# Pooled attention into a rational mixture layer on one core: the first keys on 96 partitions, the first queries by halves of the heads, the first values' first addition on GpSimd, and the order of the work planned anew

## The chip, the core and the metric

The kernel runs on one NeuronCore of a Trainium2 chip. Five engines work side by side and meet only through semaphores: TensorE (PE in the profile; its weight loads are PEld), VectorE (DVE), ScalarE (ACT), GpSimd (POOL) and SyncE (SP), which here only issues transfers. Sixteen DMA engines move the data. The metric is the device time of one execution in microseconds, lower being better: the median of the runs of a kernel.

## The reference, cut to what matters

Attention over eight batches, with keys and values averaged over groups of eight rows first, and a layer with a rational function between two products after it:

```python
B, H, S, D = 8, 8, 576, 64          # Sp = S // 8 = 72 pooled rows
k_p = k.reshape(B, H, Sp, 8, D).mean(axis=3)
v_p = v.reshape(B, H, Sp, 8, D).mean(axis=3)
scores = q @ k_p.transpose(0, 1, 3, 2) / sqrt(D)
attn = exp(scores - max); attn = attn / (sum(attn) + 1e-9)
x = (attn @ v_p), heads side by side: 4608 tokens x 512
h = x @ w_in                                            # 512 -> 2048
P = a0 + a1 h + a2 h^2 + a3 h^3
Q = 1 + |b0| |h| + |b1| h^2
out = (P / (Q + 1e-6)) @ w_out                          # 2048 -> 512
```

The two weight arrays arrive as 64-bit floats and are read as pairs of 32-bit words; everything else is 32-bit.

## The kernel before, in words

The 4608 tokens are cut into 18 blocks of 256 (`NBLK`). Each block goes through three stages: attention (`attend`), then for each of 8 units `u` of 256 hidden columns the first product (`mm1`, result `ph` in a PSUM bank), the rational function (`rational`, tiles `t`, `w`, `r`, `rp`, `gh`, `gl` on ACT, DVE and POOL) and the second product (`mm2`, result `po`). Both products are made of three matmuls each on a high and a low part, so TensorE has far more work than any other engine. Each of the 18 blocks costs TensorE the same; nothing in the change adds to or takes from the products.

**What sets the order.** The functions do not issue instructions. They record operations in a `Plan`, each with an engine, an estimated cost and a due time (`plan.now`), and `solve` then builds one list: at each step the engine that can start first takes, among the operations that could start within `LOOK` of the earliest, the one due first. `slack`, `early`, `lead`, `HEAD`, `SLOW`, the offsets of `plan.now` in `attend`'s and `mm1`'s calls are the planner's rules; changing one can move instructions everywhere. `issue` then writes every engine's instructions in that order, all on one line of the file (L299 before, L303 after), so the profile is read by tile names. Each engine runs its own list strictly in order: an instruction that waits holds all that stand behind it.

**Fillers.** Where the planner expects TensorE to be idle, `issue` writes matmuls that compute nothing (L290 before, L294 after): into the bank `idle` before the first products, later additions of zero to a `po` bank. They only keep TensorE occupied.

**The head.** The first 40 us or so are special. Block 0 is computed in two halves of four heads each (`c` = 0 and 1): `first_keys(c)` loads and pools the keys of batch 0 for these heads (tile `early` at place 0 or 3, sums on DVE, transposed on PE into `pk`, copied to `kpT`), `first_half(c)` transposes the queries (`pq`, `qT`), forms the scores (`ps`), their maxima (`mx`), the exponentials (`e`), the sums (`sm`), the product `e*sm` on POOL, and the transposed weights (`pm`, `pr`, tiles `am`); `values(0)` multiplies by the pooled values (`pv`, split into a high and a low `x`). `prep_v_early(0)` loads the values of batch 0 in two halves (`early` at place 2), adds the upper half of each row group to the lower, and sums the other steps on PE (`pvs`, and `pvr` for the remaining rows). Block 1 needs batch 0 too, block 2 needs the keys and values of batch 1 (`prep_k(1)`, `prep_v_early(1)`: the later `early`, `pk`, `pvs`, `pvr`). In between the weights are loaded (`rwin`, `rwout`), decoded (`m_win` on ACT and DVE) and split (`win`: the high part on ACT, the low one on POOL).

In this trace SyncE's queue has one ring of transfers for all of this, issued in the order of the list.

Of the kernel before, what the change touches and what calls it, by code (L numbers as in the profile page):

```python
# [100 lines left out]
class Plan:  # L101
# [8 lines left out]
    LOOK = 0.02  # L110
# [6 lines left out]
    def __init__(self, nc):  # L117
        self.nc, self.ops, self.rings, self.now, self.slack = nc, [], {}, 0.0, 2.4
# [10 lines left out]
    def add(self, eng, cost, calls, port=False, claims=(), bytes=0, early=38, after=()):  # L129
        op = Op()  # L130
        op.eng, op.cost, op.port, op.calls, op.bytes = eng, cost, port, calls, bytes
        op.early, op.slack, op.lead = early, self.slack, 0.0
        op.seq, op.due, op.deps, op.users = len(self.ops), self.now, set(), []
        touched = {}
        for _, args, kw in calls:
            every = list(args) + list(kw.values())
            dst = kw.get("out", args[0] if args else None)
            for v in every:
                if isinstance(v, Lazy) and v is not dst:
# [4 lines left out]
            if isinstance(dst, Lazy):  # L144
# [174 lines left out]
def tile_pooled_attention_then_rational_moe(  # L319
# [21 lines left out]
    G = 8  # L341
# [8 lines left out]
    SQ = 4  # L350

# [23 lines left out]
    def bank(name, shape):  # L375
        return new("ps", "ps", shape, F32, name)
# [3 lines left out]
    gp = Engine(plan, "pool", 0.242, 2.021)  # L380

# [125 lines left out]
    def prep_k(n):  # L507
# [5 lines left out]
        for c0, c1, np in ((0, 2, P), (2, 4, P), (4, 5, H * SP - 4 * P)):  # L513
# [25 lines left out]
            turned.lead = 0.75 if n > 2 else 0.0  # L539
# [18 lines left out]
    def first_keys(c):  # L558

        place = early(0, 3 * c)[:SP].rearrange("p (h x) -> p h x", h=4)  # L560
        dma(4 * SP * 2, place, k[0, 4 * c:4 * c + 4].rearrange("h (s t) d -> s h (t d)", t=G))
        pk = bank(f"pk0_{c}", [P, 2, SP])
        w = RW // 2
        while w > D:
            dve(4 * w, port=True).tensor_tensor(
                out=place[:, :, 0:w], in0=place[:, :, 0:w], in1=place[:, :, w:2 * w], op=ALU.add)
            w //= 2
        ks = new("work1", "ks", [P, 2, 2, D], F32, f"ks0_{c}")[:SP].rearrange(
            "p a b d -> p (a b) d")
# [5 lines left out]
        act(2 * SP).activation(kpT[0][0:D, js, 0:SP], pk[0:D], AF.Copy, scale=1.0 / G)  # L575
        dve(2 * SP).tensor_scalar(out=kpT[0][D:P, js, SP:2 * SP], in0=pk[D:P], scalar1=1.0 / G,
                                  scalar2=None, op0=ALU.mult)
# [5 lines left out]
    def prep_v_early(n):  # L583
# [5 lines left out]
        if n == 0:  # L589
            for c in range(2):  # L590
                js = slice(2 * c, 2 * c + 2)
                half = early(0, 2)[:, c * CW:(c + 1) * CW].rearrange("p (j x) -> p j x", j=2)
                dma(512, half, rows[js, REM:, :].rearrange("j r x -> r j x"))
                dve(RW, port=True).tensor_tensor(
                    out=half[:, :, 0:RW // 2], in0=half[:, :, 0:RW // 2],
                    in1=half[:, :, RW // 2:RW], op=ALU.add)
                for t in range(0, G // 2, 2):
                    pe(430, [mm(vs[:, js], ident, half[:, :, s * D:(s + 1) * D], s == 0,
                                s == G // 2 - 1) for s in range(t, t + 2)], claims=(vs,))
        else:  # L600
# [10 lines left out]
        w = RW // 2 if n == 0 else 0  # L611
# [4 lines left out]
        if n == 0:  # L616
            pe(250, [mm(vrs, fourfold, st[:, 0], True, True)])
        for s in range(0, G if n else 0, 2):
# [155 lines left out]
    def first_half(c, hi, lo, qt, qT, es):  # L774

        js = slice(2 * c, 2 * c + 2)
        mx = new("work2", "mx", [P, H], F32, f"mx0_{c}").rearrange(
            "p (j t h) -> p j t h", t=2, h=2)
        sm = new("work2", "sm", [P, H], F32, f"sm0_{c}")
        for t in range(2):  # L780
            pq = bank(f"pq0_{t}_{c}", [P, 2, P])
            pe(110 * 2, [
                ("transpose", (pq[:, j, :], qt[t][:, 4 * c + 2 * j:4 * c + 2 * j + 2, :].rearrange(
# [5 lines left out]
               claims=(es, mx, sm))  # L789
            dve(4 * SP).tensor_reduce(out=mx[:, :, t, :],  # L790
                                      in_=ps.rearrange("p (j h) s -> p j h s", h=2),
                                      op=ALU.max, axis=AX.X)
# [3 lines left out]
                in1=mx[:, :, t, :].unsqueeze(3).to_broadcast([P, 2, 2, SP]), op=ALU.subtract)  # L796
        act(8 * SP).activation(es[:, js], es[:, js], AF.Exp, scale=D ** -0.5)
        e = es[:, js].rearrange("p j t (h s) -> p (j t h) s", s=SP)
        dve(8 * SP).tensor_reduce(out=sm, in_=e, op=ALU.add, axis=AX.X)
# [56 lines left out]
    def attend(i):  # L856
# [64 lines left out]
    def mm1(i, u, xs):  # L921
# [5 lines left out]
        for h, cs in enumerate(parts):  # L927
            plan.now += 8 * h
# [8 lines left out]
        plan.now -= 8 * h  # L937
# [90 lines left out]
    order += [(i, u) for u0 in (0, NA) for i in (2, 3) for u in range(u0, u0 + NA)]  # L1028
# [19 lines left out]
    for at, (i, u) in enumerate(order):  # L1048
        again = i < 2 and u >= NA
        plan.now = due(at)  # L1050
        if (i, again) not in xs:
            plan.slack = 1.4
            plan.now = due(at) - (0 if again else {1: 9, 2: 8, 3: 11}.get(i, 0.0))
# [3 lines left out]
            if i < 2 and not again:  # L1057

                plan.now = due(at + 6)
# [7 lines left out]
        plan.now = due(at + LAG) + 3  # L1067
# [45 lines left out]
```

## Time and profile before

| | |
|---|---|
| median of 3 runs | 940.88 us (940.12 to 941.06) |
| the profiled execution | 941.77 us, of it the span that the trace covers 940.1 us |
| instructions in the trace | 17117 |
| DVE, ACT, POOL busy, share of the span | 81%, 72%, 56% |
| granted TensorE clock, mean | 0.998 |

A row of the timeline gives start and length in us, engine, line, operation, output and inputs, shape, a count, and in brackets the engine's idle time just before it with what ended it. A row of the windows gives for one stretch the busy time of each engine, then the granted clock (1.00 is full), the mean busy share of the DMA engines and the rate of the transfers.

### The profile page before, as it was taken

The numbers are of one execution on the slowest core, as the hardware profiler recorded it, in microseconds if no ns is written. First come the engines' busy times: TensorE is split into PE (matmuls) and PEld (weight loads), VectorE is DVE, ScalarE is ACT, GpSimd is POOL, SyncE is SP. The second block draws the span as 40 slices with busy tenths as digits, with TensorE's granted clock in tenths as the row PEclk, the third lists the DMA queues.
The fourth block names the chain that finished last, engine by engine and source line by source line (L and its number), as shares of the span: only waits on it lengthen the run. The fifth ranks groups of instructions, "written<-read, shape, count | busy, mean of one in ns | idle before, by whom it ended". The sixth has DMA issues, their size and how long they took to land.

```text
span 940.1 us, 17117 instructions
## 1 busy us (share of the span) xinstructions
PE 929.1 (99%) x6158; PEld 845.3 (90%) x6158; DVE 763.6 (81%) x1335; ACT 677.6 (72%) x1126; POOL 530.8 (56%) x474
## 2 busy tenths in 40 slices
PE   7999999999999999999999999999999999999998
PEld 7899999989999999999999899999999899999996
DVE  6889987688879777878888788878886988787764
ACT  3788888667677767776776867686867786777764
POOL 5776788685447544445644574457543754444452
PEclk9999999999999999999999999999999999999999
DMA  9995201163233412122603160215212231202000
GB/s 282 306 378 176 46 29 46 40 161 87 47 79 76 115 24 58 26 59 51 141 9 70 41 155 10 39 41 129 69 27 53 68 80 23 57 1 58 1 23 23
DMA packets 185072, 75.32 MB, mean 80 GB/s; under 512 B 162332, under 2 KB 162332, under 8 KB 184988
## 3 DMA queue, kind: packets, MB, share of 16 engines
q1 hardware_dynamic: 184988, 74.23, 30.9%
q8 instruction: 49, 0.80, 0.4%
q14 instruction: 35, 0.29, 0.1%
HBM read 50.59 MB, written 12.58 MB: 67 GB/s over the span
## 4 chain that ended last, share of the span: by engine, by line
PE 95%; DMA 3%; SPq 2%; issue 0%; ACT 0%
PE po L299 43%; PE ph L299 43%; PE pv L299 4%; PE ps L299 4%; SPq L299 2%; DMA early<-in_v_dram 1%; DMA q<-in_q_dram 1%; PE pvs L299 1%; PE pk L299 0%; PE pvr L299 0%; PE pq L299 0%; PE pm L299 0%; PE po L290 0%; PE pr L299 0%; PE pl L299 0%
## 5 line engine op out<-in xcount | busy, mean ns | idle before, releaser
L299 PEld LDWEIGHTS ph<-x,win 128*128 128x128 f32 x3264 | 484.4, 188 | 61.7 <-DVE x L299 0.5
L299 PE MATMUL ph<-x,win 128*128 128x256 f32 x3264 | 507.5, 282 | 0.5 <-DVE x L299 0.3
L299 PE MATMUL po<-wout,gh 128*128 128x512 f32 x1152 | 356.9, 396 | 0.0
L299 POOL TENSOR_TENSOR w<-w,r 128x512 f32<-128x512 f32 (+1 forms) x145 | 193.8, 1336 | 269.9 <-ACT r L299 268.2
L299 POOL TENSOR_TENSOR gl<-t,gh 128x512 fp32r<-128x512 f32 (+1 forms) x145 | 190.8, 1316 | 79.5 <-ACT gh L299 78.2
L299 PEld LDWEIGHTS po<-wout,gh 128*128 128x128 f32 x1152 | 182.3, 189 | 7.8 <-issue 0.4
L299 PE MATMUL po<-wout,gl 128*128 128x512 f32 x576 | 181.7, 396 | 0.0
L299 DVE SCALAR_TENSOR_TENSOR t<-t,abn,rp 128x512 f32<-128x512 f32 (+1 forms) x145 | 106.9, 738 | 51.8 <-ACT rp L299 50.0
L299 ACT ACTIVATE t<-ph,abn 128x512 f32<-128x512 f32 (+1 forms) x145 | 112.2, 774 | 40.7 <-PE ph L299 30.2
L299 DVE TENSOR_TENSOR t<-t,ph 128x512 f32<-128x512 f32 (+1 forms) x145 | 97.8, 676 | 41.9 <-ACT t L299 41.0
L299 ACT ACTIVATE r<-w,abn 128x512 f32<-128x512 f32 (+1 forms) x145 | 117.7, 812 | 13.3 <-POOL gl L299 6.6
L299 ACT ACTIVATE w<-ph 128x512 f32<-128x512 f32 (+1 forms) x145 | 86.1, 594 | 54.8 <-PE ph L299 34.8
L299 ACT ACTIVATE rp<-w 128x512 f32<-128x512 f32 (+1 forms) x145 | 86.6, 597 | 41.8 <-POOL w L299 40.1
L299 ACT CAST gh<-t 128x512 fp32r<-128x512 f32 (+1 forms) x145 | 88.8, 613 | 37.7 <-DVE t L299 36.9
L299 DVE SCALAR_TENSOR_TENSOR t<-t,abn,ph 128x512 f32<-128x512 f32 (+1 forms) x145 | 106.4, 735 | 2.4
L299 DVE SCALAR_TENSOR_TENSOR t<-rp,t 128x512 f32<-128x512 f32 (+1 forms) x145 | 98.4, 679 | 2.4
L299 DVE SCALAR_TENSOR_TENSOR rp<-w,rp 128x512 f32<-128x512 f32 (+1 forms) x145 | 98.8, 681 | 0.3
L299 PEld LDWEIGHTS po<-wout,gl 128*128 128x128 f32 x576 | 89.5, 188 | 2.2 <-issue 0.2
L299 ACT ACTIVATE rp<-rp 128x512 f32<-128x512 f32 (+1 forms) x145 | 84.1, 580 | 2.6
L299 POOL TENSOR_TENSOR e<-e,sm 128x576 f32<-128x576 f32 x36 | 42.0, 1186 | 20.4 <-DVE sm L299 14.3
L299 PE MATMUL pv<-am,vm 128*128 128x256 f32 (+3 forms) x288 | 45.9, 279 | 0.0
L299 PEld LDWEIGHTS pv<-am,vm 128*128 128x128 f32 x288 | 41.9, 192 | 0.4
(109 smaller groups left out, 849.6 us busy)
## 6 DMA issues: line engine op xcount, KB each, us to landing
am<-e SPq DMA_DIRECT2D x224, 48.0 KB, 2.1
out_dram<-ob SPq DMA_DIRECT2D x17, 512.0 KB, 3.1
rwin<-in_moe_w_in_dram SPq DMA_DIRECT2D x8, 1024.0 KB, 10.1
rwout<-in_moe_w_out_dram SPq DMA_DIRECT2D x8, 1024.0 KB, 10.5
st_k<-in_k_dram SPq DMA_DIRECT2D x12, 512.0 KB, 4.7
st_v<-in_v_dram SPq DMA_DIRECT2D x12, 512.0 KB, 3.9
q<-in_q_dram SPq DMA_DIRECT2D x144, 32.0 KB, 1.9
st_v<-in_v_dram SPq DMA_DIRECT2D x48, 64.0 KB, 2.2
```

Source lines behind the costliest of these rows:

```text
L299: getattr(engines[op.eng], name)(*map(value, args), **{k: value(v) for k, v in kw.items()})
```

## The change

**The keys of `first_keys`.** Before, a half's 4 heads x 72 pooled rows lie on 72 partitions, four pieces of 2 KB each from four places. Now the 288 rows are dealt to 96 partitions, three consecutive rows of 2 KB (6 KB in one piece) on each. The additions run over 3 rows instead of 4; the last one writes each sum twice side by side (`twice`), three transposes of 96 columns replace two of 72, and the two copies into `kpT` read with a stride of three.

**Block 0's queries.** Two transfers of all 8 heads (one for each 128 tokens) become four of 4 heads.

**The first values' first addition** moves from DVE to GpSimd (`V1E`); the count of matmuls after it is the same.

**The planner.** `LOOK` 0.02 to 0.04, `slack` 2.4 to 2.2 in the beginning, `early` 38 to 54, one `lead` 0.75 to 0.25, and the due times of blocks 1 to 3, of the spills, of the second half of `mm1` and of the rational function. The first maxima get tiles of their own. Options that are added and stay off (`EXPS`, `V1BS`, `REST`, `ORD`) build nothing.

```diff
-    LOOK = 0.02
+    LOOK = 0.04
...
-        self.nc, self.ops, self.rings, self.now, self.slack = nc, [], {}, 0.0, 2.4
+        self.nc, self.ops, self.rings, self.now, self.slack = nc, [], {}, 0.0, 2.2
...
-    def add(self, eng, cost, calls, port=False, claims=(), bytes=0, early=38, after=()):
+    def add(self, eng, cost, calls, port=False, claims=(), bytes=0, early=54, after=()):
...
+    MODE = 0, 1, 0
+    ORD, EXPS = 0, 0
+    V1BS, REST = 0, 0
...
+    V1B = [(), (gp,), (dve,), (gp, gp), (gp, dve)][V1BS]
+    K1E, V1E, K1W = (dve, gp)[MODE[0]], (dve, gp, None)[MODE[1]], (D, RW // 4, RW // 2)[MODE[2]]
...
-            turned.lead = 0.75 if n > 2 else 0.0
+            turned.lead = 0.25 if n > 2 else 0.0
...
     def first_keys(c):
-        place = early(0, 3 * c)[:SP].rearrange("p (h x) -> p h x", h=4)
-        dma(4 * SP * 2, place, k[0, 4 * c:4 * c + 4].rearrange("h (s t) d -> s h (t d)", t=G))
-        pk = bank(f"pk0_{c}", [P, 2, SP])
-        w = RW // 2
+        rows = 4 * SP // 3
+        place = early(0, 3 * c)[:rows, 0:3 * RW].rearrange("p (r x) -> p r x", r=3)
+        dma(2 * 4 * SP, place, k[0, 4 * c:4 * c + 4].rearrange(
+            "h (s t) d -> (h s) (t d)", t=G).rearrange("(p r) x -> p r x", r=3), run=6144)
+        pk = bank(f"pk0_{c}", [P, 3, rows])
+        w, adder = RW // 2, (dve, K1E)[c]
         while w > D:
-            dve(4 * w, port=True).tensor_tensor(
+            adder(3 * w, port=True).tensor_tensor(
                 out=place[:, :, 0:w], in0=place[:, :, 0:w], in1=place[:, :, w:2 * w], op=ALU.add)
             w //= 2
-        ks = new("work1", "ks", [P, 2, 2, D], F32, f"ks0_{c}")[:SP].rearrange(
-            "p a b d -> p (a b) d")
-        dve(4 * w, port=True).tensor_tensor(
-            out=ks, in0=place[:, :, 0:w], in1=place[:, :, w:2 * w], op=ALU.add)
-        pe(110 * 2, [("transpose", (pk[:, j, :], ks[:, 2 * j:2 * j + 2, :].rearrange(
-            "p h d -> p (h d)"), ident[:SP, :SP]), {}) for j in range(2)])
+        twice, both = place[:, :, 2 * D:4 * D], [rows, 3, 2, D]
+        adder(6 * D, port=True).tensor_tensor(
+            out=twice.rearrange("p r (m d) -> p r m d", m=2),
+            in0=place[:, :, 0:D].unsqueeze(2).to_broadcast(both),
+            in1=place[:, :, D:2 * D].unsqueeze(2).to_broadcast(both), op=ALU.add)
+        pe(110 * 3, [("transpose", (pk[:, r], twice[:, r], ident[:rows, :rows]), {})
+                     for r in range(3)])
...
-                dve(RW, port=True).tensor_tensor(
-                    out=half[:, :, 0:RW // 2], in0=half[:, :, 0:RW // 2],
-                    in1=half[:, :, RW // 2:RW], op=ALU.add)
+                if V1E:
+                    V1E(RW, port=True).tensor_tensor(
+                        out=half[:, :, 0:RW // 2], in0=half[:, :, 0:RW // 2],
+                        in1=half[:, :, RW // 2:RW], op=ALU.add)
...
             def start(c):
                 first_keys(c)
-                for t in range(2 - 2 * c):
-                    dma(2 * P, qt[t], q[0, :, t * P:(t + 1) * P, :].rearrange("h s d -> s h d"),
-                        run=256)
+                hs = slice(4 * c, 4 * c + 4)
+                for t in range(2):
+                    dma(P, qt[t][c], q[0, hs, t * P:(t + 1) * P, :].rearrange(
+                        "h s d -> s h d"), run=256)
...
-            plan.now = due(at) - (0 if again else {1: 9, 2: 8, 3: 11}.get(i, 0.0))
+            plan.now = due(at) - (0 if again else {1: 12, 2: 6, 3: 12}.get(i, 0.0))
...
-                plan.now = due(at + 6)
+                plan.now = due(at + 8)
...
-        plan.now = due(at + LAG) + 3
+        plan.now = due(at + LAG) + 5
```

Over the whole program the instructions are the same but for these: 81 fillers into `idle` become 75, 14 additions of zero to `po` become 1, 4 transposes into `pk` become 6, two additions go from DVE to POOL, and the transfers of the first keys and queries are cut as told.

What the new plan moves shows on three engines. The first place is SyncE's list at the start; `early_0` and `early_3` are the first keys, `early_1` the remaining rows of the values (16 partitions) and `early_2` the values' two halves. Before:

```order
L299 DMA early_0_96<-in_k_dram 72x4x512
L299 DMA early_3_98<-in_k_dram 72x4x512
L299 DMA q_106<-in_q_dram 128x8x64 x2
L299 DMA early_1_116<-in_v_dram 16x2x512 x2
L299 DMA early_2_127<-in_v_dram 128x2x512
L299 DMA rwin_134<-in_moe_w_in_dram 128x4x512
L299 DMA early_2_127<-in_v_dram 128x2x512
L299 DMA rwin_156<-in_moe_w_in_dram 128x4x512
L299 DMA fourfold<-in_moe_a_dram 1x4
L299 DMA rwin_212<-in_moe_w_in_dram 128x4x512
L299 DMA rwout_225<-in_moe_w_out_dram 128x2x1024
L299 DMA q_236<-in_q_dram 128x8x64 x2
```

After:

```order
L303 DMA early_0_96<-in_k_dram 96x1536
L303 DMA early_3_98<-in_k_dram 96x1536
L303 DMA q_105<-in_q_dram 128x4x64 x4
L303 DMA early_1_126<-in_v_dram 16x2x512 x2
L303 DMA early_2_140<-in_v_dram 128x2x512 x2
L303 DMA rwin_162<-in_moe_w_in_dram 128x4x512
L303 DMA rwin_196<-in_moe_w_in_dram 128x4x512
L303 DMA fourfold<-in_moe_a_dram 1x4
L303 DMA rwin_214<-in_moe_w_in_dram 128x4x512
L303 DMA q_225<-in_q_dram 128x8x64 x2
L303 DMA rwout_241<-in_moe_w_out_dram 128x2x1024
```

The second half of the values now goes ahead of the first weights, and block 1's queries (`q_236`, now `q_225`) ahead of the first `rwout`.

The second place is POOL from the end of its masks to block 1's softmax; `e_249` and `e_250` are block 0's weights, `e_497` and `e_459` block 1's. Before:

```order
L299 TENSOR_TENSOR early_1_116<-early_1_116 32x4x2x64
L299 TENSOR_TENSOR early_1_116<-early_1_116 32x2x2x64
L299 TENSOR_TENSOR early_1_116<-early_1_116 32x2x64
L299 TENSOR_TENSOR e_249<-e_249,sm_0_276 128x576
L299 TENSOR_TENSOR e_249<-e_249,sm_1_317 128x576
L299 TENSOR_TENSOR win_359<-m_win_274,win_359 128x1024
L299 TENSOR_TENSOR win_441<-m_win_353,win_441 128x1024
L299 TENSOR_TENSOR early_0_272<-early_0_272 128x2x256 x2
L299 TENSOR_TENSOR win_471<-m_win_419,win_471 128x1024
L299 TENSOR_TENSOR e_497<-e_497,sm_526 128x4x144
```

After:

```order
L303 TENSOR_TENSOR early_1_126<-early_1_126 32x4x2x64
L303 TENSOR_TENSOR early_1_126<-early_1_126 32x2x2x64
L303 TENSOR_TENSOR early_2_140<-early_2_140 128x2x256 x2
L303 TENSOR_TENSOR early_1_126<-early_1_126 32x2x64
L303 TENSOR_TENSOR e_250<-e_250,sm_0_278 128x576
L303 TENSOR_TENSOR e_250<-e_250,sm_1_297 128x576
L303 TENSOR_TENSOR win_361<-m_win_300,win_361 128x1024
L303 TENSOR_TENSOR win_453<-m_win_356,win_453 128x1024
L303 TENSOR_TENSOR early_0_260<-early_0_260 128x2x256 x2
L303 TENSOR_TENSOR e_459<-e_459,sm_491 128x4x144
```

The values' two additions stand ahead of block 0's first `e*sm`, and the third `win` no longer stands ahead of block 1's `e*sm`.

The third place is PE's list around block 1's transposed weights (`pm_591` before, `pm_550` after). Before:

```order
L299 MATMUL ph_2_552<-x_0_405,win_471 128x256 x8
L299 MATMUL ph_2_552<-x_0_412,win_471 128x256 x4
L299 MATMUL pm_591<-identr,e_497 128x128 x4
L299 MATMUL ph_2_552<-x_0_405,win_471 128x256 x4
L299 MATMUL pm_604<-identr,e_497 128x128 x4
L299 MATMUL pr_613<-identr,e_497 128x128 x2
L299 MATMUL pr_623<-identr,e_497 128x128 x2
L299 MATMUL pvs_629<-early_2_433,identr 128x256 x4
L299 MATMUL pv_0_646<-am_1_602,vm_324 128x256
```

After:

```order
L303 MATMUL ph_1_486<-x_0_402,win_453 128x256 x4
L303 MATMUL ph_1_486<-x_0_414,win_453 128x256 x2
L303 MATMUL ph_1_486<-x_0_402,win_453 128x256 x2
L303 MATMUL pm_550<-identr,e_459 128x128 x4
L303 MATMUL pm_565<-identr,e_459 128x128 x4
L303 MATMUL pr_574<-identr,e_459 128x128 x2
L303 MATMUL pr_584<-identr,e_459 128x128 x2
L303 MATMUL pv_0_598<-am_1_563,vm_330 128x256
```

The 24 matmuls of block 0's third unit (`ph_2`), which stood ahead of and between block 1's transposes, now follow block 1's values; and batch 1's first matmuls on its values (`pvs`) no longer stand ahead of block 1's `pv`.

More of the change, by code (lines that the diff above doesn't have):

```diff
@@ L136, in add @@
             every = list(args) + list(kw.values())
-            dst = kw.get("out", args[0] if args else None)
+            dsts = [kw.get("out", args[0] if args else None)]
+            if "accum_out" in kw:
+                dsts.append(kw["accum_out"])
             for v in every:
-                if isinstance(v, Lazy) and v is not dst:
+                if isinstance(v, Lazy) and not any(v is d for d in dsts):
                     box = v.box()
@@ L143, in add @@
                     touched[id(v.tile)] = v.tile
-            if isinstance(dst, Lazy):
+            for dst in dsts:
+                if not isinstance(dst, Lazy):
+                    continue
                 t, box = dst.tile, dst.box()
@@ new lines, in first_keys @@
+        adder(6 * D, port=True).tensor_tensor(
[4 more added lines that the diff above has]
+                     for r in range(3)])
+        js = slice(2 * c, 2 * c + 2)
+        for hh in range(2):
+            half = slice(hh * D, (hh + 1) * D)
+            to = kpT[0][half, js, hh * SP:(hh + 1) * SP].rearrange("p c (x r) -> p c x r", r=3)
+            src = pk[half].rearrange("p r (c h x) -> p h c x r", c=2, h=2)[:, hh]
+            if hh == 0:
+                act(2 * SP).activation(to, src, AF.Copy, scale=1.0 / G)
+            else:
+                dve(2 * SP).tensor_scalar(out=to, in0=src, scalar1=1.0 / G, scalar2=None,
+                                          op0=ALU.mult)
@@ L615, in prep_v_early @@
             w //= 2
-        if n == 0:
+        if n == 0 or REST:
             pe(250, [mm(vrs, fourfold, st[:, 0], True, True)])
-        for s in range(0, G if n else 0, 2):
+        for s in range(0, 0 if n == 0 or REST else G, 2):
             pe(500, [mm(vrs, fourfold, st[:, t], t == 0, t == G - 1) for t in range(s, s + 2)])
@@ L788, in first_half @@
                             kpT[0][:, 2 * c + j, :], True, True) for j in range(2)],
[L789 to L792, printed above, removed]
+               claims=(es, sm))
+            mx = new("work2", "mx", [P, 4], F32, f"mx0_{c}_{t}")
+            dve(4 * SP).tensor_reduce(out=mx, in_=ps, op=ALU.max, axis=AX.X)
+            if EXPS:
+                dve(4).tensor_scalar(out=mx, in0=mx, scalar1=-D ** -0.5, scalar2=None,
+                                     op0=ALU.mult)
+                for j in range(2):
+                    for h in range(2):
+                        n = 4 * j + 2 * t + h
+                        act(SP + 60).activation(
+                            es[:, 2 * c + j, t, h * SP:(h + 1) * SP], ps[:, 2 * j + h, :], AF.Exp,
+                            bias=mx[:, 2 * j + h:2 * j + h + 1], scale=D ** -0.5,
+                            accum_out=sm[:, n:n + 1])
+                continue
             dve(4 * SP).tensor_tensor(
@@ L795, in first_half @@
                 in0=ps.rearrange("p (j h) s -> p j h s", h=2),
-                in1=mx[:, :, t, :].unsqueeze(3).to_broadcast([P, 2, 2, SP]), op=ALU.subtract)
-        act(8 * SP).activation(es[:, js], es[:, js], AF.Exp, scale=D ** -0.5)
+                in1=mx.rearrange("p (j h) -> p j h", h=2).unsqueeze(3).to_broadcast(
+                    [P, 2, 2, SP]), op=ALU.subtract)
         e = es[:, js].rearrange("p j t (h s) -> p (j t h) s", s=SP)
-        dve(8 * SP).tensor_reduce(out=sm, in_=e, op=ALU.add, axis=AX.X)
+        if not EXPS:
+            act(8 * SP).activation(es[:, js], es[:, js], AF.Exp, scale=D ** -0.5)
+            dve(8 * SP).tensor_reduce(out=sm, in_=e, op=ALU.add, axis=AX.X)
         dve(0).tensor_scalar(out=sm, in0=sm, scalar1=1e-9, scalar2=None, op0=ALU.add)
@@ L927, in mm1 @@
         for h, cs in enumerate(parts):
-            plan.now += 8 * h
+            plan.now += 5 * h
             for f in range(2):
@@ L936, in mm1 @@
                         for c in cs], after=last),
-        plan.now -= 8 * h
+        plan.now -= 5 * h
         return ph
@@ L1027, in tile_pooled_attention_then_rational_moe @@
     order = [(0, 0), (0, 1), (1, 0), (0, 2), (1, 1), (0, 3), (1, 2), (1, 3)]
-    order += [(i, u) for u0 in (0, NA) for i in (2, 3) for u in range(u0, u0 + NA)]
+    order += [(i, u) for i in (2, 3) for u in range(NA)]
+    order += [[(i, u) for i in (2, 3) for u in range(NA, NU)],
+              [(2, 4), (2, 5), (3, 4), (2, 6), (3, 5), (2, 7), (3, 6), (3, 7)],
+              [(i, u) for u in range(NA, NU) for i in (2, 3)]][ORD]
     order += [(i, u) for i in range(2) for u in range(NA, NU)]
```

33 lines of the change are left out of this document (17 added, 16 removed).

## Prediction

> **What bounds the kernel now.** I read the page's head first, then the chain that ended last, TensorE's waits, and windows cut at the places that those name.
>
> ```profile
> span 940.1 us, 17117 instructions
> PE 929.1 (99%) x6158; PEld 845.3 (90%) x6158; DVE 763.6 (81%) x1335; ACT 677.6 (72%) x1126; POOL 530.8 (56%) x474
> PE 95%; DMA 3%; SPq 2%; issue 0%; ACT 0%
> ```
>
> TensorE is busy for 99% of the span and carries 95% of the chain. So only time in which it waits, runs at a lower clock or runs fillers can be won. Its waits:
>
> ```profile
> PE pq L299 <- DMA q<-in_q_dram: 2.9, 2, 2.6
> PE pvs L299 <- DMA early<-in_v_dram: 1.0, 1, 1.0
> PE pr L299 <- ACT e L299: 0.5, 1, 0.5
> PE ph L299 <- DVE x L299: 0.3, 1, 0.3
> PE ph L299 <- ACT x L299: 0.2, 1, 0.2
> ```
>
> These are total, count and longest; all lie in the first 44 us, as the windows show (columns: PE, PEld, DVE, ACT, POOL busy, clock, DMA share, GB/s).
>
> ```profile
> 1.00:2.00 1.00, 0.00 (x0) 0.00 (x0) 0.58 (x1) 1.00 (x1) 0.93 (x8) 1.00 0.43 33
> 2.00:3.00 1.00, 0.79 (x3) 0.79 (x4) 0.47 (x3) 0.09 (x1) 1.00 (x10) 1.00 0.46 78
> 3.00:4.00 1.00, 1.00 (x7) 1.00 (x6) 0.00 (x0) 0.00 (x0) 0.97 (x10) 1.00 0.73 268
> 4.00:5.00 1.00, 1.00 (x7) 1.00 (x6) 0.00 (x0) 0.00 (x0) 1.00 (x11) 1.00 0.85 201
> 9.00:10.00 1.00, 0.00 (x0) 0.00 (x0) 0.39 (x1) 0.00 (x0) 0.00 (x0) 1.00 1.02 215
> 16.00:17.00 1.00, 1.00 (x9) 1.00 (x10) 0.71 (x3) 1.00 (x3) 0.00 (x0) 1.00 1.06 412
> 40.30:43.71 3.41, 1.88 (x12) 1.43 (x12) 2.79 (x6) 3.29 (x10) 3.41 (x5) 1.00 1.28 171
> 43.71:47.12 3.41, 3.41 (x12) 2.88 (x11) 1.63 (x3) 0.98 (x2) 2.58 (x3) 0.50 1.02 372
> 79.25:900.00 820.75, 820.75 (x5433) 747.58 (x5433) 679.74 (x1182) 600.67 (x989) 462.05 (x378) 1.00 0.26 59
> ```
>
> From 79.25 to 900 TensorE has no gap, and the change leaves its matmuls there the same in number. The result is decided before 80 us. There it loses time in four ways: everything until the first `ph`, the waits around block 1, a stretch of 3.41 us at half clock (1.7 us lost), and fillers.
>
> **1. The start, until the first `ph`.** The path is keys, additions on DVE, scores, softmax, `pv`, `x`.
>
> ```profile
> 10.40 0.65 PE L299 MATMUL pq<-identr,q 128*128 128x128 f32 x4 [2.62 <-DMA q<-in_q_dram]
> 12.87 0.70 PE L299 MATMUL ps<-kpT,qT 128*128 128x144 f32 x4
> 26.17 0.50 PE L299 MATMUL ph<-x,win 128*128 128x256 f32 x2 [0.23 <-ACT x L299]
> ```
>
> ```profile
> 6.26 1.94 DVE L299 TENSOR_TENSOR early<-early 72x1024 f32<-72x1024 f32 x2 [3.66 <-DMA early<-in_k_dram]
> 9.61 1.22 DVE L299 TENSOR_TENSOR early<-early 72x1024 f32<-72x1024 f32 x1 [1.41 <-DMA early<-in_k_dram]
> 11.88 0.42 DVE L299 TENSOR_TENSOR ks<-early 72x256 f32<-72x256 f32 x1
> 14.10 0.46 DVE L299 TENSOR_TENSOR e<-ps,mx 128x288 f32<-128x288 f32 x1
> 15.93 0.68 DVE L299 TENSOR_TENSOR early<-early 128x512 f32<-128x512 f32 x1
> 18.54 0.64 DVE L299 TENSOR_TENSOR early<-early 128x512 f32<-128x512 f32 x1
> ```
>
> The first keys are there at 6.26, the second at 9.61, and PE starts on queries at 10.40. By 5.00 the windows have moved 33+78+268+201 = 580 KB, about the first keys (590 KB), so landing takes some 1.25 us more. While keys are alone (3 to 4) the DMA share is 0.73 at 268 GB/s; with full-width weights it is 1.06 at 412. That leaves two readings: a quarter of the engines has no keys, or the stream is still starting.
>
> The Trainium skill (DMA: Bandwidth & Descriptors, "Why a DMA increments its semaphore by 16 and not by 1") has the first: a transfer uses the largest number of engines up to 16 that divides its partitions, so 72 give 12 and 96 give 16. The 0.73 agrees with 12 of 16; no run so far shows 96. By it the keys' 1.18 MB take 2.9 us instead of 3.9; by the other reading nothing.
>
> Bounds: at worst the keys stream as before and the 256-byte pieces of the queries set the time (gain 0 from the transfers). At best the keys go first at the rate of 16 to 17: 111 KB are moved by 3.0, the remaining 1.07 MB take 2.6 us, to 5.6; the queries (0.52 MB) follow at the 215 GB/s of 9 to 10, 2.4 us, to 8.0, landed at 9.3. I take the best end less a little, since the row at 3 to 4 is nearest: there the keys ran alone, as they now do throughout. The first keys then land near 5.4, the second near 6.9. An addition over 288 columns takes 0.46 and over 512 0.68, so 1.0 ns a column: 768 columns take about 0.94, 384 about 0.55, and a half 2.0 instead of the 2.3 of 1024, 512 and 256. DVE's list runs both halves through by 9.4 (its last four additions are queued behind one another); from the last addition's end (12.30) to the first scores 0.57 passed, and with one more transpose I count 0.7, which puts them at 10.1 instead of 12.87, 2.8 us earlier. Only the first two of the four query transfers are needed for the first scores, and all four land by 9.3.
>
> From the first scores to the first `ph` passed 13.3 us. DVE loses the two additions of the values (0.68, 0.64) there. Against that, block 1's first `pq` now stands ahead of `ph` in PE's list and waits for its own transfer; ahead of `rwout` it comes 1 MB earlier, about 2.5 us. I take half a microsecond for that. The first `ph` then starts at 23.9: **-2.3 us**, bounds 0 and -2.9.
>
> GpSimd takes the two additions in a gap:
>
> ```profile
> 18.77 1.42 POOL L299 TENSOR_TENSOR e<-e,sm 128x576 f32<-128x576 f32 x1 [3.41 <-DVE sm L299]
> 22.48 1.15 POOL L299 TENSOR_TENSOR e<-e,sm 128x576 f32<-128x576 f32 x1 [2.29 <-ACT vm L299]
> 29.78 2.93 POOL L299 TENSOR_TENSOR win<-m_win,win 128x1024 fp32r<-128x1024 f32 x1 [2.63 <-ACT win L299]
> 32.67 2.54 POOL L299 TENSOR_TENSOR early<-early 128x512 f32<-128x512 f32 x2
> 38.00 2.26 POOL L299 TENSOR_TENSOR e<-e,sm 128x576 f32<-128x576 f32 x2 [0.43 <-DVE sm L299]
> ```
>
> Two such additions take 2.54, and POOL was idle for 3.41 before the first `e*sm`. Cost 0, as long as the values land in that gap; if they do not, `e*sm`, `pm` and all of `pv` are queued behind them (a rival below). Putting the values' second half ahead of the first weights delays `rwin` by 0.5 MB, 1.3 us, which the earlier stream covers.
>
> **2. Block 1's hand-over.**
>
> ```profile
> 39.26 0.61 PE L299 MATMUL pm<-identr,e 128*128 128x128 f32 x4
> 40.31 0.66 PE L299 MATMUL pm<-identr,e 128*128 128x128 f32 x4
> 41.84 0.33 PE L299 MATMUL pr<-identr,e 128*128 128x128 f32 x1 [0.55 <-ACT e L299]
> 43.16 3.22 PE L299 MATMUL pvs<-early,identr 128*128 128x256 f32 x8 [0.99 <-DMA early<-in_v_dram]
> 45.82 0.99 PE L299 MATMUL pv<-am,vm 128*128 128x256 f32 x2
> ```
>
> ```profile
> 41.01 0.59 ACT L299 CAST am<-pm 128x512 fp32r<-128x512 f32 x1
> ```
>
> Before, PE needed 13.1 us from its first `ph` to `pm`, 0.5 of it waiting. The new list has 20 matmuls of `ph_2` fewer (2.2 us) and four `pq` fewer (0.4) in this stretch, so PE is at `pm` near 23.9 + 10.1 = 34.0. POOL's `e*sm` no longer has the third `win` (2.4) ahead: its additions on batch 1's keys end at 35.2 - 2.3 = 32.9, the two products at 34.05 and 35.2. PE waits hardly at all for the first and 0.7 for the second; then `pr` waits for ACT's copies and `pv` for DVE's subtractions, which before lay under `pvs`. With casts of 0.59 and subtractions of 0.68 (512 columns, as the additions above) and about 0.4 (256) one after the other `pv` starts near 37.9. Of these 3.9 us PE works about 1.6, so it waits 2.3 instead of 0.55 + 0.99; 0.4 more for `ph` on its way. **+1.2 us**; bounds 0 (the copies keep up) and +2.5 (nothing of it covered). The `pvs` behind them wait for values that land 2 to 3 us earlier than 43.0, about when PE comes, which I count at nothing.
>
> **3. The clock.** From 40.30 to 43.71 PE was busy for 1.88 of 3.41 us, much of it transposes, and the next 3.41 us ran at 0.50. The new stall is as long, so I carry the same loss: **0**; bounds -1.7 (no such stretch) and +1.7 (two).
>
> **4. The additions of zero to `po`.**
>
> ```profile
> 76.50 0.61 PE L290 MATMUL po<-zero,identr 128*128 128x256 f32 x4
> 76.94 0.60 PE L299 MATMUL pm<-identr,e 128*128 128x128 f32 x4
> ...
> 78.76 0.58 PE L290 MATMUL po<-zero,identr 128*128 128x256 f32 x3
> ```
>
> There are four such groups with 14 in all, the first and the last are shown. Four take 0.44 to the next instruction, so 14 take about 1.5 us; 13 go. They are won where PE has other work in hand: by the windows it never waits after 44 us, and the new list gives it block 1 earlier. **-1.4 us**, bounds 0 and -1.5. Of the other six fillers that go, five stand in the first wait for queries, where the transfer sets the end; the sixth and the two added transposes, 0.1 us each, are inside point 1.
>
> **The sum.** -2.3 + 1.2 + 0 - 1.4 = -2.5 us. The profiled execution took 941.77 us, its span 940.1; it stands 0.89 above the median of 940.88. The forecast for the median is 940.88 - 2.5 = **938.4**.
>
> **Rivals.**
> - *The transfers gain nothing.* The small pieces of the queries, and the idle share at 3 to 4 as a start-up, speak for it; the share of 0.73 against it. Only shorter additions are left, 0.5 us: -0.5 + 1.2 - 1.4 = -0.7, 940.2.
> - *No stretch at half clock.* If block 1's waits fall across two windows of the clock's control, the 1.7 us are won on top: 936.7. The Trainium skill (TensorE: Matmul & The Clock Gate, "What's actually happening") would have it so always, since it halves the clock after an idle window of about 3.4 us and this stall holds work; but 1.88 busy of 3.41 was enough here, so the trace speaks for the loss.
> - *GpSimd becomes the bound at block 0.* The first `e*sm` cannot start before the values' second half has landed plus 1.27 and a short addition (0.5); the second starts 1.3 later, 3.0 after the landing, and the first `ph` came 3.7 after that (22.48 to 26.17). With the landing by 17 nothing is lost. At 21.6 the first `ph` is at 28.3 instead of 23.9: 938.4 + 4.4 = 942.8, slower by 0.2%. Before, that half was there by 18.54 behind 1 MB of weights that it now precedes, so this is unlikely.
>
> **Chances.** 0.48 for the forecast (its own range 937.4 to 939.8), 0.20 for transfers that gain nothing, 0.20 for no half clock, 0.06 for GpSimd, 0.06 for what I have not seen, half on each side. No change cannot be told from 0.2%, 1.9 us: below 939.0 is faster, above 942.8 slower. Faster: two thirds of the forecast's share, 0.32, with 0.20 and 0.03, 0.55. Same: 0.16 + 0.20, 0.36. Slower: 0.06 + 0.03, 0.09. The range 936.2 to 941.8 leaves out GpSimd's case and the unseen ones.
>
> **What would show it.** Point 1: a DMA share near 1 from 3 to 5 us, first `ps` near 10.1, first `ph` near 23.9; POOL's two additions done before its first `e*sm`, which follows DVE's `sm`. Point 2: waits of `pm` for POOL and `pv` for DVE near 34 to 38 us, 2 to 3 us together. Point 3: one stretch of 3.41 us at 0.50 right after. Point 4: no gap on PE where the additions of zero were. The forecast is wrong if the first `ph` stays at 26, if PE waits again past 45 us, or if the clock falls a second time.

## The result, and the profile after

The changed kernel took 947.62 us, the median of seven runs (942.52 to 948.18); the kernel before took 941.06 on the same chip (940.12 to 941.65). The ratio is 1.0059, with a 95% interval of 1.004 to 1.0078: slower by 0.6%, where 938.4 was forecast. The quickest of the seven runs, 942.52, had a mean clock of 0.999; the other six, at 0.994 to 0.996, took 945.12 to 948.18. The profiled execution took 948.18 us, its span is 946.5 us against 940.1.

TensorE's waits in the changed kernel (total us, count, longest):

```profile
PE pq L303 <- DMA q<-in_q_dram: 1.9, 1, 1.9
PE ph L303 <- DVE x L303: 1.8, 1, 1.8
...
PE pk L303 <- DVE ks L303: 1.5, 1, 1.5
PE pv L303 <- DVE am L303: 1.0, 1, 1.0
PE pl L303 <- DVE ks L303: 0.8, 1, 0.8
PE pm L303 <- POOL e L303: 0.5, 1, 0.5
PE ph L303 <- DVE t L303: 0.4, 1, 0.4
PE pr L303 <- ACT e L303: 0.4, 1, 0.4
PE po L303 <- ACT gh L303: 0.2, 1, 0.2
```

Waits for `ks`, `t` and `gh` are new. They lie in the long stage in which TensorE never waited before. The windows of this execution, the slowest of the seven, say how much (PE, PEld, DVE, ACT, POOL busy, granted clock, DMA share, GB/s):

```profile
3.00:4.00 1.00, 1.00 (x6) 1.00 (x6) 0.00 (x0) 0.00 (x0) 0.97 (x11) 1.00 1.05 344
4.00:5.00 1.00, 1.00 (x6) 1.00 (x6) 0.00 (x0) 0.00 (x0) 1.00 (x11) 1.00 0.97 246
...
5.49:8.90 3.41, 1.55 (x12) 1.28 (x11) 2.50 (x4) 0.00 (x0) 2.40 (x10) 1.00 1.21 214
8.90:12.31 3.41, 3.31 (x17) 2.75 (x16) 2.09 (x5) 1.07 (x4) 1.07 (x1) 0.50 1.07 304
12.31:15.73 3.42, 3.42 (x16) 3.42 (x15) 2.08 (x5) 1.17 (x4) 3.34 (x5) 0.50 1.05 408
...
39.62:43.03 3.41, 1.72 (x10) 1.17 (x10) 2.99 (x6) 3.41 (x12) 3.41 (x5) 1.00 1.04 275
43.03:46.45 3.42, 3.38 (x16) 3.39 (x17) 3.08 (x4) 2.58 (x6) 1.29 (x3) 0.50 1.02 404
79.25:900.00 820.75, 817.64 (x5408) 744.71 (x5407) 685.48 (x1178) 601.44 (x986) 457.87 (x376) 1.00 0.27 60
```

Three things are to be read here. From 3 to 4 us the keys move at 344 GB/s with a DMA share of 1.05, where it was 268 and 0.73: the transfers gained, though in the next microsecond they move at 246, and the forecast had counted with 412. The clock is halved from 8.90 to 15.73, two windows, after a window in which TensorE was busy for 1.55 of 3.41 us; before, it was whole from 6.17 to 43.71. And from 79.25 to 900 TensorE stands still for 820.75 - 817.64 = 3.1 us, where before it stood still for none.

The start on TensorE (start, busy time, instruction, and the idle time before it with what ended it):

```profile
8.47 0.44 PE L303 MATMUL pq<-identr,q 128*128 128x128 f32 x2 [1.86 <-DMA q<-in_q_dram]
...
11.95 1.16 PE L303 MATMUL ps<-kpT,qT 128*128 128x144 f32 x4
...
27.00 0.50 PE L303 MATMUL ph<-x,win 128*128 128x256 f32 x2
29.27 0.51 PE L303 MATMUL ph<-x,win 128*128 128x256 f32 x2 [1.77 <-DVE x L303]
```

The queries are there 1.9 us earlier than before (8.47 against 10.40), the first scores 0.9 earlier, but a group of four takes 1.16 instead of 0.70, and the first `ph` comes 0.8 us later than before (27.00 against 26.17). The next pair waits for `x`. Why `x` and `ks` are late is seen only when VectorE and GpSimd are laid side by side:

```profile
19.78 0.64 DVE L303 TENSOR_SCALAR m_win<-m_win 128x1024 int32<-128x1024 int32 x1
...
25.08 2.39 POOL L303 TENSOR_TENSOR win<-m_win,win 128x1024 fp32r<-128x1024 f32 x1 [3.65 <-ACT win L303]
25.16 2.86 DVE L303 TENSOR_SCALAR m_win<-m_win 128x1024 int32<-128x1024 int32 x1
28.54 0.68 DVE L303 TENSOR_TENSOR x<-pv,x 128x512 fp32r<-128x512 f32 x1
...
288.27 1.26 POOL L303 TENSOR_TENSOR gl<-t,gh 128x512 fp32r<-128x512 f32 x1 [0.27 <-ACT gh L303]
288.32 1.49 DVE L303 TENSOR_TENSOR ks<-st_k 128x256 f32<-128x256 f32 x1
...
539.34 1.27 POOL L303 TENSOR_TENSOR gl<-t,gh 128x512 fp32r<-128x512 f32 x1 [0.34 <-POOL ks L303]
539.38 1.38 DVE L303 TENSOR_TENSOR ks<-st_k 64x128 f32<-64x128 f32 x1
```

Each time GpSimd's instruction began 0.04 to 0.08 us ahead of VectorE's, and VectorE's ends 0.1 to 0.6 us after it. The same `m_win` step takes 0.64 at 19.78, and the quickest `ks` additions of these two shapes 0.42 and 0.28. So VectorE seems held for the whole of GpSimd's instruction.

All fourteen profiles of this case together bear it out: of the `m_win` steps of this kind, 79 began while GpSimd ran no instruction on two tensors (`TENSOR_TENSOR`) and took 0.64 to 0.70; 33 began while it ran one, and each of the 33 ended after it. Of the `ks` additions of 128x256, 84 that began alone took 0.41 to 0.43, and all 56 that began beside such an instruction ended after it. The Trainium skill (SBUF — State Buffer, "Who interferes with whom") has the rule: the two share a pair of ports under an exclusive lock, and whoever issues first keeps it for its whole instruction; on VectorE it bears on `tensor_scalar` in its fast mode and on instructions with two inputs in SBUF. The rows agree.

### The profile page after: what moved, and what is told of

Same layout as the page of the kernel before. It is cut to its first block, busy times and chain, and to the rows that moved or that the text cites. A ratio compares the mean times of both kernels' runs of the same rounds, so it can differ in the third digit from the quotient of the medians.

```text
span 946.5 us, 17116 instructions
## 1 busy us (share of the span) xinstructions
PE 932.4 (99%) x6141; PEld 848.2 (90%) x6141; DVE 771.5 (82%) x1333; ACT 680.5 (72%) x1126; POOL 527.1 (56%) x476
## 4 chain that ended last, share of the span: by engine, by line
PE 88%; SPq 3%; DVE 3%; ACT 2%; DMA 2%; POOL 1%; issue 1%; ACTq 0%; POOLq 0%
PE ph L303 39%; PE po L303 38%; PE pv L303 4%; PE ps L303 4%; SPq L303 3%; DMA q<-in_q_dram 1%; DMA st_v<-in_v_dram 1%; PE pvs L303 1%; DVE t L303 1%; DVE sm L303 1%; ACT rp L303 0%; DVE ks L303 0%; PE pk L303 0%; DVE m_win L303 0%; POOL st_v L303 0%
## 5 line engine op out<-in xcount | busy, mean ns | idle before, releaser
L303 POOL TENSOR_TENSOR w<-w,r 128x512 f32<-128x512 f32 (+1 forms) x145 | 190.1, 1311 | 262.9 <-ACT r L303 261.4
L303 POOL TENSOR_TENSOR st_v<-st_v 128x512 f32<-128x512 f32 (+1 forms) x36 | 36.4, 1021 | 12.5 <-DMA st_v<-in_v_dram 12.1
```

The source lines that it names most:

```text
L303: getattr(engines[op.eng], name)(*map(value, args), **{k: value(v) for k, v in kw.items()})
```

## The experiments

The theory: (a) GpSimd's instruction holds VectorE's where it starts a moment earlier, and in the new list such meetings fall on instructions that TensorE waits for; (b) a standstill of TensorE can be followed by 3.41 us or more at half clock. Rivals: the new start is hidden behind something else; the planner's nine numbers are worse in themselves; a part of the change is. Times are medians; the ratio is to the kernel before, run on the same chip.

**e1_fill: no standstill at the start.**

```
+ if first transpose of q: issue 16 fillers into idle
```

> The changed kernel with 16 fillers more in front of the first query transpose, nothing moved. In the changed kernel TensorE's fillers end at 6.61, it stands still until 8.47, and the granted clock is 0.50 from 8.90 to 15.73. If that half clock costs time: the stretch is gone, a group of four ps takes 0.70 again instead of 1.16, the first ph starts at 25 to 26 instead of 27.0, and the time falls by 1.5 to 3 us, to 944.6 to 946.1. Rival, the start is hidden behind VectorE's m_win and x: the clock is whole but the first ph stays within 0.4 us of 27.0 and the second pair at 29.3, time 947.6 within 1 us. Third: the earlier start lets VectorE's m_win go ahead of GpSimd's win addition by chance, and the 1.8 us wait for x goes as well: 943 to 944.5.

943.77 us (941.65 to 946.39), ratio 1.0027 [1.0016, 1.0037]: 3.9 us less than the changed kernel.

```profile
8.14:11.56 3.42, 2.69 (x20) 1.96 (x20) 2.92 (x6) 1.03 (x3) 0.44 (x1) 1.00 1.16 274
38.86:42.28 3.42, 2.16 (x17) 1.96 (x18) 3.14 (x6) 3.42 (x10) 3.08 (x5) 1.00 1.16 265
42.28:45.69 3.41, 3.41 (x25) 3.21 (x24) 3.37 (x6) 2.85 (x6) 2.78 (x3) 1.00 1.01 398
```

```profile
11.29 0.65 PE L308 MATMUL ps<-kpT,qT 128*128 128x144 f32 x4
24.62 0.50 PE L308 MATMUL ph<-x,win 128*128 128x256 f32 x2
26.88 0.51 PE L308 MATMUL ph<-x,win 128*128 128x256 f32 x2 [1.76 <-DVE x L308]
```

The clock is whole at the start, the scores take 0.65 again and the first `ph` starts 2.4 us earlier, which answers the rival. The gain is above the range given for it. In this profile, of a run of 942.29, the clock does not fall at block 1 either; four runs at a clock of 1.00 took 941.65 to 943.26, the other eight, at 0.998 and 0.999, 943.43 to 946.39. The wait for `x` stays as long: it has another cause.

**e2_swap: one instruction of VectorE moved.**

```
- m_win1 (first step), am, x      on VectorE
+ am, x, m_win1 (first step)
```

> The changed kernel with one instruction moved on VectorE: the first decoding step of the second weights (m_win, 128x1024, 2.86 us at 25.16 where the same instruction takes 0.64 elsewhere) stands behind the first x instead of ahead of am and x. If it was held by GpSimd's win addition (25.08 to 27.47): x ends near 26.5, the 1.77 us wait of ph for x is gone or under 0.3, and the time is 1.3 to 2 us less, 945.6 to 946.3. Rival, x is late for another reason (pv and the second am): ph still waits over 1 us for x, time 947.6 within 0.6. In both m_win itself takes 0.7 or so, since GpSimd's addition has ended by then, unless it meets the next one.

944.75 us (944.3 to 945.52), 1.0038 [1.0026, 1.005].

```profile
23.73 2.40 POOL L309 TENSOR_TENSOR win<-m_win,win 128x1024 fp32r<-128x1024 f32 x1 [3.29 <-ACT win L309]
25.63 0.69 DVE L309 TENSOR_TENSOR x<-pv,x 128x512 fp32r<-128x512 f32 x1 [0.37 <-ACT x L309]
26.24 0.68 DVE L309 TENSOR_SCALAR m_win<-m_win 128x1024 int32<-128x1024 int32 x1
```

Away from GpSimd's addition `m_win` takes 0.68, not 2.86, and the wait for `x` is 0.22. So moving the step ends the wait, and with the count over all profiles above, (a) holds for this place. The gain of 2.9 us is more than the wait; in this profile the half clock at the start also lasted one window, not two, and there was none at block 1. A second loss shows in the same profile, at the wait for `ks`, which was 1.9 us here:

```profile
282.39:285.81 3.42, 1.47 (x11) 1.18 (x10) 3.20 (x5) 2.45 (x5) 2.56 (x2) 1.00 0.00 0
285.81:289.22 3.41, 3.41 (x13) 2.92 (x14) 2.60 (x7) 1.76 (x4) 1.07 (x2) 0.50 0.42 111
```

One wait in the middle of the run, and the clock falls behind it: 1.7 us on top. The changed kernel's wait at the same place was not followed by a fall.

**e3_lead: more room between `ks` and its transposes.**

```
- turned.lead = 0.25 if n > 2 else 0.0
+ turned.lead = 0.75 if n > 2 else 0.0
```

> The changed kernel with the allowance between ks and its transposes back at 0.75 us from 0.25; TensorE's list is unchanged up to the first block that needs the third keys, some 100 us in, and the transposes stand two or four products later from there. The changed kernel waits 1.5 + 0.8 us for ks (288, 440 and 539 us), 3 us by spacing of starts; VectorE's ks additions take 1.49, 1.0 and 1.38 there where others take 0.28 to 0.42. If the smaller allowance made these waits: they fall below 0.8 us together though a ks addition still takes over 1 us here or there; 1.5 to 3 us less, 944.6 to 946.1. Rival, the waits are a matter of where the new list happens to put ks beside GpSimd's additions, whatever the allowance: as long in sum as before, 947.6 within 1.

943.78 us (942.37 to 947.05), 1.0031 [1.0018, 1.0045].

```profile
PE pk L303 <- DVE ks L303: 1.5, 1, 1.5
```

Half of it: the waits for `ks` near 440 and 540 us are gone, that near 286 is as long as it was, since GpSimd's instruction (1.3) is longer than the allowance. The time also holds a start with one window less at half clock (first `ph` at 26.29) and none at block 1, so the 3.8 us are not the allowance's alone.

**e4_oldplan, e6_newplan, e7_keys: the parts of the change.** e4 is the changed kernel with the planner's nine old numbers; e6 the kernel before with the nine new ones; e7 the kernel before with the new first keys alone.

```
e4: LOOK 0.04 -> 0.02, slack 2.2 -> 2.4, early 54 -> 38, lead 0.25 -> 0.75,
    5 * h -> 8 * h, {1: 12, 2: 6, 3: 12} -> {1: 9, 2: 8, 3: 11},
    due(at + 8) -> due(at + 6), due(at + LAG) + 5 -> + 3
e6: the same lines of the kernel before, the other way
e7: first_keys of the changed kernel, additions on VectorE
```

> The changed kernel (keys on 96 partitions, queries by halves, values' addition on GpSimd) with all nine numbers of the planner put back to those before. If the loss comes from the new numbers: no wait behind 80 us, and what the transfers win stays: 938 to 940.5. If it comes from the new start itself (fillers that end early, half clock, GpSimd's and VectorE's additions in each other's way): 944 to 947, with a half clock stretch before 16 us and a first ph after 26.

> The kernel before with nothing but the nine new numbers of the planner. If the new numbers alone carry the loss: 944 to 947, with waits of PE for ks behind 200 us. If they carry half of it, by the smaller allowance: 942 to 944. If they are harmless without the new start, or take away fillers in po (13 of 14, 1.4 us): 939 to 941.

> The kernel before with the first keys alone changed: 96 partitions of three rows, three transposes. If the shorter transfer and additions are a gain by themselves: the first keys' addition starts near 5.6 instead of 6.26, the first ps near 11.5 instead of 12.87 (the queries, not by halves, then set it), 939 to 940.5. If a plan laid out for another start loses again to GpSimd's and VectorE's additions in each other's way, or to the half clock: 942 to 946, with one wait over 1 us at an instruction of VectorE that takes two to four times its usual time.

e4: 945.82 us (944.07 to 948.6), 1.0049 [1.0034, 1.0063]. e6: 944.39 (942.53 to 946.59), 1.0035 [1.0023, 1.0048]. e7: 944.69 (941.83 to 951.22), 1.0047 [1.0026, 1.0068]. The new start with the old numbers loses, the new numbers with the old start lose, and so do the new keys alone: each of these three plans is 3 to 5 us slower than the kernel before, so the loss belongs to no one part, and each has it at other places. e4's waits:

```profile
PE pv L303 <- DVE am L303: 3.1, 2, 2.1
...
PE ph L303 <- DVE x L303: 1.8, 1, 1.8
...
PE po L303 <- POOL gl L303: 1.1, 1, 1.1
```

In e6's profile TensorE waits 2.9 us for the first queries and two windows at half clock follow; from 79.25 to 900 it stands still for 1.8 us (820.75 - 819.00):

```profile
6.37:9.78 3.41, 1.51 (x13) 1.31 (x11) 1.91 (x2) 0.00 (x0) 0.37 (x6) 1.00 0.99 185
9.78:13.20 3.42, 2.38 (x12) 2.38 (x13) 2.89 (x5) 0.66 (x2) 0.02 (x1) 0.50 0.97 210
```

And e7's windows around block 1, where `pm`, `pv` and `pvs` wait one after the other:

```profile
38.18:41.59 3.41, 1.58 (x11) 1.06 (x10) 2.98 (x6) 2.84 (x8) 3.41 (x4) 1.00 1.25 200
41.59:45.01 3.42, 1.75 (x4) 1.17 (x4) 2.32 (x3) 1.43 (x4) 0.53 (x1) 0.50 1.13 283
45.01:48.42 3.41, 3.41 (x12) 2.79 (x12) 0.85 (x2) 1.31 (x3) 0.65 (x2) 0.50 1.03 412
```

The half clock lasted four windows there, to 55.25. Over e7's runs the time goes with the mean clock: 941.8 to 943.3 at 1.00, 946.1 to 951.2 at 0.991 to 0.996.

**e5_all: the three mends together.**

```
+ e1's 16 fillers, e2's order on VectorE
- turned.lead = 0.25 if n > 2 else 0.0
+ turned.lead = 2.0 if n > 2 else 0.0
```

> The changed kernel with the 16 fillers ahead of the first query transpose, m_win's first step behind the first x, and the allowance between ks and its transposes at 2.0 us, more than a whole GpSimd addition (1.3). If the three losses are separate (half clock 3.9, m_win held by GpSimd 2.9, ks held by GpSimd up to 3.8 with the clock that falls after it, less what two of them share): 937.5 to 939.5, faster than the kernel before, first ph near 24.6 and no wait for x or ks over 0.3. If the planner's new list with the larger allowance only puts other instructions in each other's way: 940 to 943, with new waits of PE behind 100 us.

941.33 us (940.14 to 942.24), 1.0002 [0.9994, 1.0011]: 6.3 us less than the changed kernel and level with the one before, 2 to 4 us above what the three should give. With 2.0 us of room the held `ks` costs nothing:

```profile
284.48 1.52 DVE L314 TENSOR_TENSOR ks<-st_k 128x256 f32<-128x256 f32 x1
```

```profile
286.09 0.40 PE L314 MATMUL pk<-identr,ks 128*128 128x128 f32 x2
```

The addition is held as before, and the transposes come when it is done, without a wait. In this profile, of one of the slowest of the eleven runs, a queries' transfer came 1 us later (first `pq` at 9.44), a half clock followed after all (11.39 to 14.80), and two steps of VectorE that add 1e-9 to the softmax sums, held, took 1.27 and 1.07 instead of 0.16. The half clock is not most of what is missing to the expectation: eight of the runs had a mean clock of 0.999 or 1.00 and took 940.14 to 941.67. More of it is in the products themselves, which take 1.7 us more than in the kernel before (819.4 against 817.7, counted as in the account below).

**e8_bfill: fillers in the kernel before.** 22 of them, at the same place.

> The kernel before with 22 fillers more ahead of the first query transpose, in the 2.62 us that TensorE stands still there. If the half clock after a standstill also touches the kernel before in some of its runs: a part of a microsecond less, 940.0 to 941. If 2.62 us of standstill behind a longer run of fillers never made the clock fall there: no change, 941.3 within 0.4. In neither case more, since no work waits behind the fillers.

942.01 us (939.74 to 942.6), 1.0006 [0.9997, 1.0015]: no gain that can be told, and a median above both of the ranges expected. Its runs fall into two groups: five of 939.7 to 941.0 at a mean clock of 0.999 and 1.00, seven of 942.0 to 942.6 at 0.997 and 0.998. The same program differs by 2 us, about one window at half clock.

**e9_best, e10_best_nosm, e12_best_am: a version that keeps the new start.** Each adds to the one before.

```
e9:  e5, with 22 fillers ahead of the first transpose of q, 3 ahead of the next two
e10: - sm = sm + 1e-9          (36 times, on VectorE)
e12: am's last subtraction of block 13 two places earlier on VectorE
```

> e5_all with more fillers at the start: 22 ahead of the first query transpose and 3 ahead of each of the next two groups of them, since in e5_all's profile the queries came a microsecond later than in the others and the clock fell at 11.39 all the same after a window of 3.41 us in which TensorE was busy for 1.58. If the window's busy time decides: no half clock before 40 us in the profile, the share of runs at a clock of 0.998 shrinks, 939.5 to 941. If the fillers delay the transposes more than the clock gives back, or the clock falls elsewhere: 941 to 942.5.

> e9_best without the 36 additions of 1e-9 to the softmax sums (each sum is at least 1 and a float32 does not change by it); nothing is planned anew. They take 0.16 us each, but 0.6 to 1.27 where GpSimd is at work, and two of them stood on the path in e5_all: ph waits 0.4 for t at 100 us behind sm of 1.27, ps 0.7 at 294 behind sm of 1.07. If VectorE is held there by GpSimd: both waits go, 0.8 to 1.4 us less than e9_best. If the next instruction on VectorE is held instead, since most of them read two operands from memory too: the waits stay, within 0.4 of e9_best.

> e10_best_nosm with one instruction of VectorE two places earlier: the last subtraction for am of block 13, ahead of t<-t,ph and t<-t,abn,ph. In e10_best_nosm it ran at 672.92 and pv waited 0.90 for it, the only wait of TensorE behind 45 us; e9_best lost 1.05 there and 1.7 more to the half clock that followed. If such a wait is worth itself and the clock after it: 1.0 to 1.5 us less, 938.8 to 939.5, faster than the kernel before by over 0.1%. If the two t steps, 0.7 us later, make a product wait instead: 940 to 940.8.

e9: 941.57 us (939.62 to 942.65), 1.0008 [0.9999, 1.0017]. No half clock at its start; but `pv` of block 13 waited 0.9 us for `am`, which stood behind other steps of VectorE, and a window at half clock followed (677.25 to 680.67). No gain over e5. e10: 940.31 (938.37 to 941.75), 0.9996 [0.9988, 1.0005]; the waits for `t` and behind `sm` are gone, and the median is 1.3 us lower; the wait of block 13's `pv` stays. e12: 939.45 (938.73 to 940.76), 0.9985 [0.9975, 0.9994], faster than the kernel before by 1.6 us. Its waits behind the first filler, and the long stage:

```profile
PE pv L323 <- DVE am L323: 1.0, 1, 1.0
PE pr L323 <- ACT e L323: 0.7, 2, 0.4
PE ph L323 <- POOL win L323: 0.4, 1, 0.4
PE ph L323 <- DVE x L323: 0.2, 1, 0.2
```

```profile
79.25:900.00 820.75, 820.73 (x5435) 749.45 (x5434) 675.56 (x1150) 602.38 (x987) 457.25 (x375) 1.00 0.26 59
```

From 79.25 to 900 TensorE stands still for 0.02 us, where it was 3.1 in the changed kernel.

**e11_before_nosm: the kernel before without the 36 steps.**

> The kernel before without the 36 additions of 1e-9, nothing planned anew. TensorE never waits behind 44 us there, so only the one sm of 1.55 us at 36.0 lies near the path (pm and pr of block 1): if it counts, 0.3 to 1 us less, and the clock falls less often at 43.7; if not, no change, within 0.4 of the kernel before.

939.75 us (939.14 to 941.61), 0.9992 [0.9983, 1.0001]: 0.8 us less, at the edge of what can be told. With the same saving on both sides the new start is worth little: against the kernel before on its own chip e12 gains 1.6 us and e11 0.8, and their intervals overlap.

## Why the prediction was wrong

**Point 1, the start (-2.3 us).** The reading of the transfers was right in kind, 344 GB/s at a share of 1.05 in place of 268 at 0.73. The Trainium skill (DMA: Bandwidth & Descriptors, "Why a DMA increments its semaphore by 16 and not by 1") gives 16 engines for 96 partitions, and the share agrees. The size was wrong. The forecast took the weights' 412 GB/s for all of the keys; they moved at 344 and then at 246, and the additions on the two halves start at 5.88 and 7.92, where 5.4 and 6.9 were forecast and 6.26 and 9.61 were before:

```profile
5.88 1.55 DVE L303 TENSOR_TENSOR early<-early 96x768 f32<-96x768 f32 x2 [3.78 <-DMA early<-in_k_dram]
7.92 2.48 DVE L303 TENSOR_TENSOR early<-early 96x768 f32<-96x768 f32 x4 [0.49 <-DMA early<-in_k_dram]
```

With the clock whole (e1) the second half starts at 8.08 and the last addition ends at 10.56 instead of 9.4. With the 0.7 that the forecast allows from there, the first scores come at 11.3; they start at 11.29, not 10.1. A second step failed at the same moment: "only the first two of the four query transfers are needed for the first scores". TensorE's list has all four groups of `pq` and both of `pk` ahead of the first `ps`, and in e1 the last queries are there at 10.61. The two came together, so the run does not tell which alone would have held the scores. The first `ph` is at 24.62 in e1: the term was -1.55, not -2.3. In the changed kernel itself it was +0.8, by the half clock, which stood under point 3.

**Not foreseen: `x`.** The first `ph` was taken as the end of the start. Behind it `x` cost 1.8 us, because VectorE met GpSimd. The rival "GpSimd becomes the bound" had the wrong place: the values' additions end at 16.15, before VectorE has the first sum, so their cost of 0 holds.

**Point 2, block 1's hand-over (+1.2).** Right in kind, too large. `pm`, `pr` and `pv` wait 0.45 + 0.38 + 0.97 = 1.8 us in place of 0.55 + 0.99: +0.3. TensorE came to `pm` at 38.94 instead of 34.0, which gave the copies more time; that this is why they were waited for less is argued, not shown. `pvs` no longer waits, as was said.

**Point 3, the clock (0).** Outside its bounds of -1.7 and +1.7. The window at block 1 stayed, and two more came at the start, where they cost 2.4 us at the first `ph` (27.00 against 24.62 in e1). The quoted rows of before held the warning: TensorE waited 2.62 us for the queries without a fall, and the forecast took away the wait but did not ask where the fillers would end. They end at 6.61 in the changed kernel, where the plan has the queries; these come at 8.47.

**Point 4, fillers in `po` (-1.4).** Right, and a little small: one is left of 14. From start to start the 14 took 1.79 us and the one takes 0.11, so 1.7 us less.

**The claim under all four.** "From 79.25 to 900 TensorE has no gap ... the result is decided before 80 us" is the step that failed most in the profiled run. That no gap was seen there was a property of one order in which no held step of VectorE fell on a product, with 0.75 us of room behind `ks`: the kernel before has a `ks` addition of 1.00 near 436 us too, and no wait. The change drew a new order and cut the room to 0.25, and its cost was put at nothing. It was 3.1 us of waits there, and the clock falls behind one of them in some plans.

**The account.** Until 79 us: start +0.8, `x` +1.5 (1.77 against 0.29), hand-over +0.3, fillers -1.7, one fall of the clock on both sides: +0.9. Behind it 3.1 us of waits. Of the 6.4 us by which the span grew, 2.4 are in none of the waits that the profile names. They lie in the spacing of the products: counted from start to start, with idle time left out, all matmuls into `ph` and `po`, as many in both kernels, take 820.25 us in the changed one and 817.70 before, 2.55 more. The forecast put this at nothing, since the matmuls are the same in number. The usual `ph` matmul is followed by the next after 118.8 ns in place of 118.1. All runs built on the changed kernel show 118.7 or 118.8, and all that were built on the one before 117.9 to 118.2, those with the new numbers (e6) and the new keys (e7) too. What spaces them apart stays open.

Also open is what makes one standstill halve the clock and not another: over all profiles, 12 of 17 windows at full clock with 1.36 to 1.98 us busy were followed by a fall, the other five not (1.61 in the kernel before, 6.17 to 9.58, is one of them), and in e9 and e12 the clock fell after windows of 2.52 and 2.16.

## What to carry to other kernels

Where a planner or a table sets the order, a changed cost anywhere draws a new order everywhere; "TensorE never waits there" is a fact about the old order, and belongs into a prediction as a risk with a price, not as a zero. Lay VectorE's and GpSimd's rows side by side and look for instructions that take several times their usual time: those are the meetings, and what helped here was more room ahead of whoever waits (2.0 us) than GpSimd's instruction takes (1.3). Fillers should end when the data really land, not when the plan has them land: behind a standstill of 1.86 us the half clock cost 2.4 us more here, though one of 2.62 in the kernel before cost nothing more.

## What the hardware showed that was not expected

The sharpness of a hold: GpSimd began 0.08 us ahead, and a `tensor_scalar` took 2.86 us instead of 0.64. The windows of the clock are 3.41 us long and begin at another moment in each run (5.49, 5.92, 6.17, 6.96, 7.41 in the profiles), and the runs of one kernel spread over 1 to 9 us; that this is by where the standstills fall in the windows fits the runs' clocks but is not shown. The Trainium skill (TensorE: Matmul & The Clock Gate, "What's actually happening") has the window of 3413 ns that runs free, and the trace agrees; its idle window as the condition does not fit, since windows with 40 to 74% of busy time were enough here. The first record of the clock in a profile is the change to full speed, at 6.17 in the kernel before and 5.49 in the changed one. The windows ahead of it print 1.00, but the fillers follow each other every 0.213 us there and every 0.120 behind it, so both begin at half clock.
